# First chunk in two halves: the values' products of two row blocks moved ahead of the queries

## The chip, the cores and the metric

One core of a Trainium2 chip runs the kernel. The metric is the device time of one execution in microseconds; the program uses no other core. Engines: TensorE (PE, matmuls and transposes; PEld its weight loads), VectorE (DVE), ScalarE (ACT), GpSimd (POOL) and SyncE (SP, which here only issues DMAs).

## What is computed

```python
def _A_ref(x, wqkv, wo):                      # full attention, S=2048, D=512, 32 heads of 16
    qkv = (x @ wqkv) ...                      # q, k, v
    p = softmax(einsum(q, k) * Dh ** -0.5)
    return einsum(p, v) ... @ wo

def _B_ref(x, w1, b1, w2, b2):                # token mixer, F=1792
    h = layernorm(x)
    u = gelu(einsum("bsd,sf->bdf", h, w1) + b1)
    return transpose(einsum("bdf,fs->bds", u, w2) + b2)

xn = layernorm(x)
out = x + _A_ref(xn, A_wqkv, A_wo) * silu(_B_ref(xn, B_w1, B_b1, B_w2, B_b2))
```

All tensors are float32.

## The kernel before

The whole kernel has one order, written out by hand: each engine, and each DMA queue, takes its instructions in the order in which the program issues them. Every product is made of three: operands are split into an upper part (`wh`, or index 0 of a tile), rounded to the reduced float32 format, and a lower part (`wl`, index 1), the rest, and upper by upper, upper by lower and lower by upper are added in PSUM. ACT makes upper parts by a cast, DVE (from PSUM) or GpSimd (from SBUF) makes lower parts by a subtraction (`sub`, line 76).

The first stage works on the 2048 rows of x in four chunks of 512 rows, each of four row blocks of 128. For a chunk it does the following.

- `load_x` (line 162) loads four blocks; `first(c)` normalises them with `Norm` (lines 193 to 231): statistics of each block (`stats`), one reciprocal root for all four (`rsqrt`, of which one step is on ACT), then the four blocks scaled (`apply`, line 219).
- `turned(c, db)` (lines 261 to 269) transposes one column block of all four row blocks on PE into one PSUM bank, and ACT (line 267) and DVE make its two parts, tile `xt`. A chunk has four column blocks, so four such tiles.
- Eight groups of twelve matmuls (line 300) make the queries (four groups) and then the keys (four). A group takes the four upper weight slices with the upper rows, then the same with the lower rows, then the four lower weight slices with the upper rows. ACT and DVE split each result into `sg` (line 305), of which there are three buffers, and it is stored. Between the groups stand two at a time the pieces of `todo`: the normalisation of the next chunk, and the second normalisation of this chunk (`second`), whose results `hx` are split by ACT (line 243) and GpSimd into `hu`, for the mixer.
- The values of four row blocks (`v_product`, lines 83 to 85) follow, 48 matmuls, with the next chunk's transposes among them. Their results go by ACT (line 354) to `v48` tiles of two buffers, in which GpSimd has set the ones (line 353), and are stored to `v_d` (line 355).

In the first chunk the weights have to be brought in as well. Twelve slices (three parts: queries 0, keys 1, values 2; four slices `kd` each) are loaded in this order (line 182) into eleven buffers, so the tenth waits until the first has been used up. `w_upper` (line 187) casts a part's slices on ACT, `w_lower` (line 191) subtracts them on GpSimd. The loads of the two bias vectors are issued behind those of chunk 1's rows (lines 289, 290), and DVE has one small operation on the second vector (`b2h`, line 291) ahead of everything that it does in the loop for chunk 0.

PSUM has eight banks, handed out in turn by `bank()`. Behind the four chunks come the mixer's products and the attention, which fill the rest of the span.

Of the kernel before, what the change touches and what calls it, by code (L numbers as in the profile page):

```python
# [8 lines left out]
F32 = mybir.dt.float32  # L9
F32R = mybir.dt.float32r  # L10
AF = mybir.ActivationFunctionType
OP = mybir.AluOpType
# [9 lines left out]
def tile_attention_token_mixer(ctx, tc, x, wqkv, wo, w1, b1, w2, b2, out):  # L22
# [128 lines left out]
    with (  # L151
        tc.tile_pool(name="pw", bufs=1) as pw,
        tc.tile_pool(name="px", bufs=5) as px,
        tc.tile_pool(name="pt", bufs=6) as pt,
        tc.tile_pool(name="pst", bufs=3) as pst,
# [29 lines left out]
        def w_upper(part):  # L185
            for kd in range(ND):
                nc.scalar.copy(wh[part][:, kd, :], raw_w[part, kd])

        def w_lower(part):
            for kd in range(ND):  # L190
                sub(nc.gpsimd, wl[part][:, kd, :], raw_w[part, kd], wh[part][:, kd, :])

        class Norm:


            def __init__(self, src, dst, then=None):
                self.src, self.dst, self.then = src, dst, then
                self.st = pst.tile([P, 4, 6], F32, name="st")
                self.mv = pst.tile([P, 4, 2], F32, name="mv")
# [5 lines left out]
            def rsqrt(self):  # L205
                ve = pst.tile([P, 4], F32, name="ve")
                r = self.r = pst.tile([P, 4], F32, name="r")
                t = pst.tile([P, 4], F32, name="t")
                nc.vector.tensor_scalar(ve, self.mv[:, :, 1], 1e-5, None, op0=OP.add)
# [16 lines left out]
            def pieces(self):  # L226
                for b in range(4):
                    yield lambda b=b: self.stats(b)
                yield self.rsqrt
                for b in range(4):  # L230
                    yield lambda b=b: self.apply(b)

        def first(c):
# [4 lines left out]
            return Norm(lambda b: xr[4 * c + b], dst)  # L238

# [15 lines left out]

        for f in first(0).pieces():
            f()
        w_upper(0)
        xts_ = [[] for _ in range(NC)]

        def turned(c, db):

            ps = bank()
            for b in range(4):
                nc.tensor.transpose(ps[:, b * P : (b + 1) * P], xn[4 * c + b][:, db * P : (db + 1) * P], ident)
            t = pt.tile([P, 2, 512], F32R, name="xt")
            nc.scalar.copy(t[:, 0, :], ps)
            sub(nc.vector, t[:, 1, :], ps, t[:, 0, :])
            xts_[c].append(t)

        for c in range(NC):
            cs = slice(c * 512, (c + 1) * 512)
            for db in range(len(xts_[c]), ND):
# [12 lines left out]
            if c == 0:  # L286
                w_upper(2)
                w_lower(2)
                nc.sync.dma_start(b1t, b1.rearrange("(b p) -> p b", p=P))
# [46 lines left out]

            pv = [bank()[:, :D] for _ in range(4)]
            if c + 1 < NC:
                for kd in range(ND):
                    for b in range(4):  # L340
# [3 lines left out]
            for b, ps in enumerate(pv):  # L344
                if c + 1 == NC:
# [4 lines left out]
                else:  # L350
                    v48 = pt.tile([P, 2, 512], F32R, name="xt").bitcast(F32).rearrange("p a b -> p (a b)")
                    v48 = v48[:, : NP * 48].rearrange("p (a b c) -> p a b c", b=3, c=DH)
                nc.gpsimd.memset(v48[:, :, 1, :], 1.0)
                nc.scalar.copy(v48[:, :, 0:3:2, :], ps.rearrange("p (a b c) -> p a b c", b=2, c=DH))
                nc.sync.dma_start(v_d[4 * c + b], v48.rearrange("p a b c -> p (a b c)"))

# [732 lines left out]
```

## Time and profile before

| | before |
|---|---|
| median of 3 runs | 1708.67 us (1707.78 to 1708.83) |
| the profiled execution's own time | 1709.11 us |
| its span in the profile | 1707.3 us |
| PE, DVE, ACT, POOL busy | 98%, 83%, 70%, 33% of the span |
| PE clock granted, mean | 0.995 |
| first transpose on PE | 9.65 us |
| first product of queries, chunk 0 | 13.61 us |
| first product of values, chunk 0 | 36.97 us |
| first product of queries, chunk 1 | 48.92 us |

The span runs from the first to the last recorded instruction; the execution's own time has some 1.8 us around it. In the timeline a row gives start, duration, engine, line and operation, `out<-in`, and in brackets how long the engine was idle before it and what ended that. Starts of neighbouring matmuls tell more than their durations, which overlap.

### The profile page before, as it was taken

Reading aid. Unit: us, or ns where it says so; the run is one execution under the profiler, and the core shown is the slowest. Engines: PE = TensorE matmul, PEld = TensorE weight load, DVE = VectorE, ACT = ScalarE, POOL = GpSimd, SP = SyncE. Lnnn points to the kernel's source line nnn. Section 1 sums busy time; section 2 is a strip of 40 time slices with the busy share of each in tenths; the row PEclk is TensorE's granted clock in tenths of the full one; section 3 lists DMA queues with packets and bytes.
Section 4 is the critical chain, followed back from the end, with each engine's and each line's share of the span. In section 5 each row is a group of like instructions: output and inputs, shape, how many; then the busy total and the mean of one; then the engine's idle time right before and its main releaser. Section 6 shows DMA issues by size and latency. Waiting matters only on the chain.

```text
span 1707.3 us, 30652 instructions
## 1 busy us (share of the span) xinstructions
PE 1672.8 (98%) x11716; PEld 846.9 (50%) x11716; DVE 1409.7 (83%) x2378; ACT 1187.9 (70%) x2291; POOL 567.1 (33%) x673
## 2 busy tenths in 40 slices
PE   7999999999999999999999999999999999999987
PEld 6887644444444444444444444444444444444443
DVE  6565888888888888888888888888888888888834
ACT  3333277777777777777777777777777777787845
POOL 4223842233342334333422322222222222463401
PEclk9999999999999999999999999999999999999999
DMA  6467611415150514353332415141515132272435
GB/s 222 179 235 184 133 44 42 75 44 85 45 85 20 92 46 68 135 127 94 75 60 64 79 35 82 36 80 31 81 33 82 37 48 52 78 158 85 147 98 186
DMA packets 150879, 152.94 MB, mean 90 GB/s; under 512 B 51452, under 2 KB 109820, under 8 KB 147660
## 3 DMA queue, kind: packets, MB, share of 16 engines
q1 hardware_dynamic: 146188, 149.97, 36.8%
q0 software_dynamic: 4544, 1.01, 0.4%
q8 instruction: 92, 1.51, 0.4%
q14 instruction: 55, 0.45, 0.1%
HBM read 100.29 MB, written 49.53 MB: 88 GB/s over the span
## 4 chain that ended last, share of the span: by engine, by line
PE 92%; DVE 5%; ACT 1%; DMA 0%; issue 0%; POOL 0%; SPq 0%; DVEq 0%; POOLq 0%
PE av L773 28%; PE dn L911 26%; PE mx L387 13%; PE sc L757 12%; DVE mxp L391 4%; PE dn L886 3%; PE mx L300 2%; PE sc L300 2%; ACT prob L762 1%; PE av L886 1%; PE av L300 1%; PE dn L300 1%; PE mx L757 1%; PE mx L402 0%; PE sc L83 0%
## 5 line engine op out<-in xcount | busy, mean ns | idle before, releaser
L391 DVE TENSOR_REDUCE mxp<-mx 128x1 f32<-128x512 f32 x2008 | 1250.5, 683 | 183.9 <-PE mx L387 97.4
L762 ACT ACTIVATE prob<-sc 128x512 f32<-128x512 f32 x2008 | 1041.8, 604 | 331.1 <-PE sc L757 252.6
L387 PE MATMUL mx<-big 48*128 48x512 f32 x2008 | 826.8, 428 | 2.1
L757 PE MATMUL sc<-big 50*128 50x512 f32 x2008 | 771.8, 428 | 3.4 <-DMA big<-m 2.0
L911 PE MATMUL dn<-hu,wh 64*128 64x512 f32 x1570 | 573.8, 406 | 0.0
L773 PE MATMUL av<-prob,vp 128*32 128x512 f32 x4096 | 546.3, 605 | 0.0
L387 PEld LDWEIGHTS mx<-big 48*128 48x128 f32 x2008 | 364.2, 186 | 221.8 <-DVE mxp L391 206.6
L757 PEld LDWEIGHTS sc<-big 50*128 50x128 f32 x2008 | 355.1, 185 | 191.7 <-ACT prob L762 173.3
L911 PEld LDWEIGHTS dn<-hu,wh 64*128 64x128 f32 x1570 | 289.3, 185 | 171.5 <-issue 145.5
L911 PE MATMUL dn<-hu,wl 64*128 64x512 f32 x786 | 316.3, 402 | 0.0
L145 POOL CAST wh<-raw 128x512 fp32r<-128x512 f32 x108 | 62.8, 582 | 327.3 <-PE dn L911 309.6
L76 POOL TENSOR_TENSOR wl<-raw,wh 128x512 fp32r<-128x512 f32 x124 | 150.3, 1215 | 38.6 <-ACT wh L147 29.9
L773 PEld LDWEIGHTS av<-prob,vp 128*32 128x32 f32 x4096 | 81.0, 108 | 150.6 <-issue 138.6
L911 PEld LDWEIGHTS dn<-hu,wl 64*128 64x128 f32 x786 | 145.9, 186 | 8.3 <-issue 0.8
L406 POOL CAST m<-f 16x128 fp32r<-16x128 f32 x32 | 9.0, 280 | 266.1 <-DVE f L405 266.1
L464 POOL TENSOR_TENSOR sq<-u 128x512 f32<-128x512 f32 x14 | 14.6, 1040 | 170.9 <-ACT u L463 170.9
L80 POOL DMA_DIRECT2D big<-m x128 | 67.7, 535 | 0.0
L762 ACT ACTIVATE prob<-mx 128x512 f32<-128x512 f32 x40 | 25.1, 627 | 29.2 <-PE sc L757 22.0
L500 POOL TENSOR_SCALAR t<-t 128x512 f32<-128x512 f32 x16 | 23.8, 1488 | 62.4 <-ACT t L497 62.4
L911 PE MATMUL dn<-wh,hu 64*128 64x512 f32 x120 | 41.6, 399 | 0.0
L76 POOL TENSOR_TENSOR hu<-hx,hu 128x512 fp32r<-128x512 f32 x16 | 20.4, 1291 | 54.6 <-ACT hu L243 54.6
L300 PE MATMUL mx<-xt,big 128*128 128x512 f32 x144 | 35.4, 395 | 0.0
(202 smaller groups left out, 1094.2 us busy)
## 6 DMA issues: line engine op xcount, KB each, us to landing
raw<-in_B_w_dram SPq DMA_DIRECT2D x104, 256.0 KB
big<-k_d SPq DMA_DIRECT2D x96, 128.0 KB
big<-q_d SPq DMA_DIRECT2D x96, 128.0 KB
q_d<-sg SPq DMA_DIRECT2D x16, 512.0 KB
k_d<-sg SPq DMA_DIRECT2D x16, 512.0 KB
num_d<-ev SPq DMA_DIRECT2D x30, 256.0 KB
u_d<-uo SPq DMA_DIRECT2D x14, 512.0 KB
hu<-u_d SPq DMA_DIRECT2D x14, 512.0 KB
```

The costliest lines, as they stand in the source:

```text
L76: eng.tensor_tensor(out=o, in0=a, in1=b.bitcast(F32), op=OP.subtract)
L80: queue.dma_start(dst.bitcast(F32), src.bitcast(F32))
L145: nc.gpsimd.tensor_copy(whs[n][:, :m, :], raws[n][:, :m, :])
L300: nc.tensor.matmul(ps, w[part][:, kd, m], xt[kd][:, z, :], start=w is wh and z == 0 and kd == 0, stop=w is wl and kd == ND - 1,)
L387: nc.tensor.matmul(ps, q[o : o + 48, r * P : (r + 1) * P], k[o : o + 48, c * 512 : (c + 1) * 512], start=True, stop=True,)
L391: nc.vector.tensor_reduce(mxp[u // 16][:, a, r % 8, c : c + 1], ps, axis=AX.X, op=OP.max)
L500: nc.gpsimd.tensor_scalar(t, t, 1.0, None, op0=OP.add)
L757: nc.tensor.matmul(ps, ks[p][o : o + 50, kb * P : (kb + 1) * P], qs[p][o : o + 50, at : at + 512], start=True, stop=True,)
L762: nc.scalar.activation(e, ps, AF.Exp, scale=scale)
L773: nc.tensor.matmul(av[32 * j : 32 * j + 32, :], vps[p][:, kb, 16 * a : 16 * a + 32], prob.pop((t, a, c)), start=kb == 0, stop=kb == NB - 1,)
L886: nc.tensor.matmul(ps, w(slice(0, P)), m(slice(0, P)), start=first, stop=last)
L911: made.append(lambda r=r, start=first and a == lead, stop=last and a != lead: nc.tensor.matmul(ps, w(r), m(r), start=start, stop=stop,))
```

## The change

The values' weights are loaded first, and split first. The first chunk's four row blocks are normalised as two pairs, each with a root of its own. Its blocks are turned one block at a time (all four column blocks of a row block into one bank) rather than one column block at a time, and cast in halves of 256 elements. Between the turns stand the values' products of the first two row blocks, 24 matmuls; then come the queries' weights, and the loop goes on as before, with values of only two blocks left at its end for chunk 0. The `xt` tiles become pairs, three buffers in place of six. The results of the two early blocks are copied and stored ahead of the bias vectors' loads.

```diff
-        tc.tile_pool(name="pt", bufs=6) as pt,
+        tc.tile_pool(name="pt", bufs=3) as pt,
...
-        for part in range(3):
+        for n, part in enumerate((2, 0, 1)):
             for kd in range(ND):
-                nm = ("raw", "wh", "wl")[(part * ND + kd) % 3]
+                nm = ("raw", "wh", "wl")[(n * ND + kd) % 3]
...
             def rsqrt(self):
-                ve = pst.tile([P, 4], F32, name="ve")
+                at = slice(self.some[0], self.some[-1] + 1)
+                ve = pst.tile([P, 4], F32, name="ve")[:, at]
...
-        for f in first(0).pieces():
-            f()
-        w_upper(0)
...
+            if db % 2 == 0:
+                t2 = pt.tile([P, 2, 2, 512], F32R, name="xt")
+                xts_[c] += [t2[:, 0], t2[:, 1]]
...
+        def block_turn(b):
+            ps = bank()
+            for db in range(ND):
+                nc.tensor.transpose(ps[:, db * P : (db + 1) * P], xn[b][:, db * P : (db + 1) * P], ident)
+            return ps
+        def block_upper(b, ps):
+            for h in range(2):
+                nc.scalar.copy(pair[h][:, :, 0, b * P : (b + 1) * P], ps[:, 256 * h : 256 * h + 256].rearrange("p (d q) -> p d q", d=2))
+        def block_lower(b, ps):
+            for h in range(2):
+                o = pair[h][:, :, :, b * P : (b + 1) * P]
+                sub(nc.vector, o[:, :, 1, :], ps[:, 256 * h : 256 * h + 256].rearrange("p (d q) -> p d q", d=2), o[:, :, 0, :])
+        def v_out(n, ps, v48, ones_in=False):
+            if not ones_in:
+                nc.gpsimd.memset(v48[:, :, 1, :], 1.0)
+            nc.scalar.copy(v48[:, :, 0:3:2, :], ps.rearrange("p (a b c) -> p a b c", b=2, c=DH))
+            nc.sync.dma_start(v_d[n], v48.rearrange("p a b c -> p (a b c)"))
...
+        halves_ = [first(0, range(2)), first(0, range(2, 4))]
+        pieces_ = [list(h.pieces()) for h in halves_]
+        for f in pieces_[0]:
+            f()
+        pair = [pt.tile([P, 2, 2, 512], F32R, name="xt") for _ in range(2)]
...
+        ps0 = block_turn(0)
+        w_upper(2, [0])
+        block_upper(0, ps0)
+        w_upper(2, [1])
+        pieces_[1][0]()
+        block_lower(0, ps0)
+        nc.gpsimd.tensor_copy(pst.tile([P, 1], F32, name="hold"), xn[1][:, :1])
+        w_lower(2, [0, 1])
+        ps1 = block_turn(1)
+        w_upper(2, [2])
+        block_upper(1, ps1)
+        w_upper(2, [3])
+        w_lower(2, [2, 3])
+        pieces_[1][1]()
+        block_lower(1, ps1)
+        for f in pieces_[1][2:]:
+            f()
+        pv = [bank()[:, :D] for _ in range(2)]
+        def v_part(b, z, w, first, last):
+            for kd in range(ND):
+                nc.tensor.matmul(
+                    pv[b], xts_[0][kd][:, z, b * P : (b + 1) * P], w[2][:, kd, :],
+                    start=first and kd == 0, stop=last and kd == ND - 1,
+                )
+        v_part(0, 0, wh, True, False)
+        v_part(0, 1, wh, False, False)
+        v_part(1, 0, wh, True, False)
+        ps2 = block_turn(2)
+        block_upper(2, ps2)
+        v_part(1, 1, wh, False, False)
+        ps3 = block_turn(3)
+        block_upper(3, ps3)
+        block_lower(2, ps2)
+        block_lower(3, ps3)
+        w_upper(0)
+        v_part(0, 0, wl, False, True)
+        v_part(1, 0, wl, False, True)
+        w_lower(0)
         for c in range(NC):
...
-            if c == 0:
-                nc.gpsimd.tensor_copy(pst.tile([P, 1], F32, name="hold"), xn[3][:, :1])
-                w_upper(1)
-                w_lower(0)
-                w_lower(1)
             xt = xts_[c]
...
             if c == 0:
-                w_upper(2)
-                w_lower(2)
+                w_upper(1)
+                w_lower(1)
+                for b in range(2):
+                    v_out(b, pv[b], v48s[b], True)
                 nc.sync.dma_start(b1t, b1.rearrange("(b p) -> p b", p=P))
                 nc.sync.dma_start(b2t, b2.rearrange("(b p) -> p b", p=P))
                 nc.vector.tensor_scalar(b2h, b2t, 0.5, None, op0=OP.mult)
...
-            pv = [bank()[:, :D] for _ in range(4)]
+            rest_ = range(2 if c == 0 else 0, 4)
+            pv = {b: bank()[:, :D] for b in rest_}
...
-                    for b in range(4):
+                    for b in rest_:
                         v_product(b, kd)
```

More of the change, by code (lines that the diff above doesn't have):

```diff
@@ L183, in tile_attention_token_mixer, with w_upper, w_lower, __init__ @@
                 raw_w[part, kd] = raw
-        def w_upper(part):
-            for kd in range(ND):
+        def w_upper(part, kds=range(ND)):
+            for kd in kds:
                 nc.scalar.copy(wh[part][:, kd, :], raw_w[part, kd])
-        def w_lower(part):
-            for kd in range(ND):
+        def w_lower(part, kds=range(ND)):
+            for kd in kds:
                 sub(nc.gpsimd, wl[part][:, kd, :], raw_w[part, kd], wh[part][:, kd, :])
         class Norm:
-            def __init__(self, src, dst, then=None):
-                self.src, self.dst, self.then = src, dst, then
+            def __init__(self, src, dst, then=None, some=range(4)):
+                self.src, self.dst, self.then, self.some = src, dst, then, some
                 self.st = pst.tile([P, 4, 6], F32, name="st")
@@ L226, in pieces, with first @@
             def pieces(self):
-                for b in range(4):
+                for b in self.some:
                     yield lambda b=b: self.stats(b)
                 yield self.rsqrt
-                for b in range(4):
+                for b in self.some:
                     yield lambda b=b: self.apply(b)
-        def first(c):
+        def first(c, some=range(4)):
             def dst(b):
@@ L236, in dst @@
                 return xn[4 * c + b]
-            return Norm(lambda b: xr[4 * c + b], dst)
+            return Norm(lambda b: xr[4 * c + b], dst, some=some)
         def second(c):
@@ new lines, in v_out @@
+        def v_out(n, ps, v48, ones_in=False):
[3 more added lines that the diff above has]
+            nc.sync.dma_start(v_d[n], v48.rearrange("p a b c -> p (a b c)"))
+        v48s = [pst.tile([P, NP, 3, DH], F32, name="v48", bufs=2) for _ in range(2)]
+        for v48 in v48s:
+            nc.gpsimd.memset(v48[:, :, 1, :], 1.0)
+        halves_ = [first(0, range(2)), first(0, range(2, 4))]
@@ new lines, in tile_attention_token_mixer @@
+        pieces_ = [list(h.pieces()) for h in halves_]
+        for f in pieces_[0]:
+            f()
+        pair = [pt.tile([P, 2, 2, 512], F32R, name="xt") for _ in range(2)]
+        xts_[0] = [pair[db // 2][:, db % 2] for db in range(ND)]
+        done_db[0] = ND
+        ps0 = block_turn(0)
[5 more added lines that the diff above has]
+        nc.gpsimd.tensor_copy(pst.tile([P, 1], F32, name="hold"), xn[1][:, :1])
@@ L271, in tile_attention_token_mixer @@
+        v_part(0, 0, wh, True, False)
[12 more added lines that the diff above has]
+        w_lower(0)
         for c in range(NC):
             cs = slice(c * 512, (c + 1) * 512)
-            for db in range(len(xts_[c]), ND):
+            for db in range(done_db[c], ND):
@@ L343, in tile_attention_token_mixer @@
                         turned(c + 1, kd + 1)
-            for b, ps in enumerate(pv):
+            for b in rest_:
                 if c + 1 == NC:
```

21 lines of the change are left out of this document (11 added, 10 removed).

## The prediction

> **What bounds the kernel now.** I read the page first (engine shares, the chain that ended last), then the timeline of the first 60 us, where all of the change lies, then the table by stretches.
>
> ```profile
> span 1707.3 us, 30652 instructions
> ...
> PE 1672.8 (98%) x11716; PEld 846.9 (50%) x11716; DVE 1409.7 (83%) x2378; ACT 1187.9 (70%) x2291; POOL 567.1 (33%) x673
> ...
> PE 92%; DVE 5%; ACT 1%; DMA 0%; issue 0%; POOL 0%; SPq 0%; DVEq 0%; POOLq 0%
> ```
>
> TensorE (PE) is busy for 98% of the span and makes up 92% of the chain that ended last. A shift of the point from which PE is busy without a break, or a gap put into it, therefore reaches the end of the kernel nearly one for one; work on other engines counts only where PE has to wait for it. Next the timeline of the start; its columns are start, duration, engine, line and operation.
>
> ```profile
> 4.97 0.18 DVE L203 BATCH_NORM_AGGREGATE mv<-st 128x2 f32<-128x6 f32 x1
> ...
> 7.29 0.18 DVE L203 BATCH_NORM_AGGREGATE mv<-st 128x2 f32<-128x6 f32 x1
> ...
> 8.96 1.92 DVE L219 TENSOR_SCALAR xn<-xr,mv,r 128x512 f32<-128x512 f32 x4
> ...
> 9.65 1.75 PE L265 MATMUL mx<-ident,xn 128*128 128x128 f32 x4 [9.65 <-DVE xn L219]
> ...
> 11.20 1.06 PE L265 MATMUL sc<-ident,xn 128*128 128x128 f32 x4
> ...
> 12.29 0.58 ACT L267 CAST xt<-sc 128x512 fp32r<-128x512 f32 x1 [0.27 <-PE sc L265]
> ...
> 13.61 3.68 PE L300 MATMUL mx<-xt,big 128*128 128x512 f32 x12
> ...
> 15.00 0.62 ACT L187 CAST big<-wl 128x512 fp32r<-128x512 f32 x1
> 15.52 0.62 ACT L187 CAST big<-raw 128x512 fp32r<-128x512 f32 x1
> ...
> 16.03 1.30 POOL L76 TENSOR_TENSOR big<-wh,big 128x512 fp32r<-128x512 f32 x1
> ...
> 17.13 2.88 PE L300 MATMUL dn<-xt,big 128*128 128x512 f32 x12
> 17.29 1.30 POOL L76 TENSOR_TENSOR big<-wl,big 128x512 fp32r<-128x512 f32 x1
> ...
> 19.85 2.88 PE L300 MATMUL av<-xt,big 128*128 128x512 f32 x12
> ```
>
> DVE computes statistics of four row blocks, the last ending with the aggregate at 7.29; the short chain for the reciprocal root follows and the four blocks are normalised from 8.96. PE's first transpose is at 9.65, the first product of queries at 13.61, the second group of twelve at 17.13, the third at 19.85. So a group costs 19.85 - 17.13 = 2.72 us, 0.227 us a matmul, while the first took 17.13 - 13.61 = 3.52 (part of it at a slow clock).
>
> From 9.65 PE has no gap up to chunk 1's first product, at 48.92:
>
> ```profile
> 36.18 0.60 PE L265 MATMUL mx<-ident,xn 128*128 128x128 f32 x4
> ...
> 36.62 0.60 PE L265 MATMUL dn<-ident,xn 128*128 128x128 f32 x4
> ...
> 36.97 0.48 PE L83 MATMUL av<-wvh,xt 128*128 128x512 f32 x1
> ...
> 45.09 0.59 ACT L267 CAST xt<-dn 128x512 fp32r<-128x512 f32 x1
> ...
> 45.56 0.60 ACT L267 CAST xt<-mx 128x512 fp32r<-128x512 f32 x1
> ...
> 46.38 0.59 ACT L267 CAST xt<-sc 128x512 fp32r<-128x512 f32 x1 [0.21 <-PE sc L265]
> ...
> 47.72 4.37 SPq L355 DMA_DIRECT2D v_d<-v  x4
> ...
> 48.92 2.88 PE L300 MATMUL mx<-xt,big 128*128 128x512 f32 x12
> 50.16 0.59 ACT L354 COPY v<-mx 128x512 f32<-128x512 f32 x1 [1.82 <-DMA v_d<-v]
> ...
> 51.13 0.58 ACT L354 COPY v<-sc 128x512 f32<-128x512 f32 x1 [0.38 <-DMA v_d<-v]
> ```
>
> The values' products of chunk 0 start at 36.97 and chunk 1's queries at 48.92. Between them lie 48 matmuls (10.9 us) and two transposed groups (1.1 us). This stretch is also where the late work of chunk 0 on DVE and ACT is hidden: the casts of chunk 1's turned rows run at 45.09, 45.56, 46.38 (the last one ready at 46.97), and PE needs the fourth of them at 48.92 + 3 x 0.227 = 49.60. The slack is 2.6 us, no more. Four transposes take 36.62 - 36.18 = 0.44 us here.
>
> **Part 1: the early start.** The first half needs two blocks only. Its last aggregate is the one at 4.97 in place of 7.29; with the same 8.96 - 7.29 = 1.67 to the first normalised block this gives 6.64, and with 9.65 - 8.96 = 0.69 PE starts at 7.33. That is 2.32 us won, if PE then runs on.
>
> It does not. Block 0's four transposes take 1.06 to the end (11.20 row) and the cast follows 0.03 later (12.29), at 8.42. ACT now has, in this order: two half casts of block 0, weight slice 1, slice 2, two half casts of block 1, slice 3. Weight casts stand 15.52 - 15.00 = 0.52 apart, whole PSUM casts 45.56 - 45.09 = 0.47. A half cast (256 elements) has no row; it lies between half of that, 0.24, and all of it, and I take 0.30, near the lower end, because the elements are halved. So slice 3 is ready at 8.42 + 4 x 0.30 + 3 x 0.52 = 11.2. The first three products slip in before; nine of the first twelve are left. At 0.227 us they end at 13.2, at the slow clock (0.453, twice that) at 15.3; I take 14.0, since the trace's own first group shows the slow clock going after some 5 us of PE work. The weights' slices load first now, so they are there no later than the queries' were. The second half is not what PE waits for: its root stands on DVE behind block 1's lower part, which follows block 1's casts, so it begins near 11.2, and PE can turn block 2 from 11.2 + 1.67 + 0.69 = 13.6. Then block 2 turned 0.44, four products 0.9, block 3 turned 0.44, eight products with the lower weights 1.8: PE is ready for the queries at 17.6.
>
> Here a wait takes the place of the old one. The cast of the queries' weights now stands on ACT behind block 3's casts (15.9 to 16.5), so its first slice is ready at 17.1; GpSimd makes the lower parts one after the other, 17.29 - 16.03 = 1.26 apart, so the fourth is there at 17.1 + 5.0 = 22.1, and the second group starts at 22.5. Before it started at 17.13: 5.4 later. Against that stand the 24 matmuls that are already done, 24 x 0.227 = 5.4. The PE side of the change is worth 0, between -0.8 and +1.3 by the two clocks.
>
> **Part 2: what is moved behind it on the queue of SP.** The stores of the first two blocks' values now stand ahead of the loads of b1 and b2, and DVE has the small operation on b2 (line 291) ahead of all its work for chunk 0.
>
> ```profile
> 15.61 0.42 SPq L289 DMA_DIRECT2D b1t<-in_B_b_dram  x1
> ...
> 16.08 3.57 SPq L290 DMA_DIRECT2D b2t<-in_B_b_dram  x1
> ...
> 22.31 1.30 DVE L291 TENSOR_SCALAR b2h<-b2t 128x16 f32<-128x16 f32 x1 [7.00 <-DMA b2t<-in_B_b_dram]
> ```
>
> DVE waited 7.00 us for b2 already, to 22.31, and only then began the subtractions of the finished groups. In the table by stretches (per engine busy us, then clock, DMA share and GB/s) b2's tiny elements show as a busy DMA share at almost no GB/s:
>
> ```profile
> 18.00:19.00 1.00, 1.00 (x6) 0.81 (x6) 0.00 (x0) 1.00 (x3) 1.00 (x2) 1.00 1.02 377
> ...
> 19.50:20.00 0.50, 0.50 (x4) 0.42 (x3) 0.00 (x0) 0.00 (x0) 0.50 (x2) 1.00 1.21 117
> ...
> 20.50:21.00 0.50, 0.50 (x4) 0.39 (x3) 0.00 (x0) 0.14 (x1) 0.50 (x1) 1.00 0.86 6
> ...
> 22.00:22.50 0.50, 0.50 (x4) 0.42 (x3) 0.19 (x1) 0.00 (x0) 0.50 (x2) 1.00 0.00 0
> ```
>
> At 18 to 19 the DMA still moves 377 GB/s of x and weights, at 19.5 to 20 a third of that, at 20.5 to 21 it is 0.86 busy at 6 GB/s, and at 22 it is idle. So b1 and b2 are moved behind the bulk ahead of them, from a little after 19 on, in about 2.9 us.
>
> After the change: ACT's eight weight casts for queries and keys last from 16.5 to 20.7, the two copies of values to about 21.7. SP issues the first store at 21.3 and the second at 21.75, b1 at 22.2, b2 from 22.65. A store issued at 47.72 had landed by 50.16 (2.44 us, the buffer's next user), and the next by 51.13, 1.0 later; so the stores are through at 21.3 + 2.44 + 1.0 = 24.7, and b2 lands at 24.7 + 2.9 + 0.3 = 27.9. DVE's backlog starts 27.9 - 22.31 = 5.6 us late. Bounds: 4.3, an estimate with ACT and the loads each some 0.65 quicker; 6.6 if b2 takes as long from b1's issue as before, 22.31 - 15.61 = 6.7, which gives 28.9; and 1.3 more at the slow clock.
>
> Who waits for that? Behind the operation on b2 are queued eight subtractions for queries and keys, all of the normalisation of chunk 1 and the second normalisation of chunk 0, then the lower parts of chunk 1's turned rows. That queue has no room:
>
> ```profile
> 30.00:36.00 6.00, 6.00 (x28) 4.95 (x28) 5.90 (x14) 1.77 (x3) 0.00 (x0) 1.00 0.73 273
> ```
>
> 5.90 of 6.00 us busy. It depends on ACT, GpSimd and its own stores, not on PE, which is ahead of it. So it moves as a block: the last cast of turned rows, ready at 46.97 before, is ready at 46.97 - 0.35 + 5.6 = 52.2 (0.35 is the wait on PE in the row of 46.38, and the tighter spacing, which fall away). PE meanwhile comes to chunk 1 at 48.9 as before: 22.5, seven groups, two turned groups, 24 matmuls instead of 48. It needs the fourth cast for its fourth product, 3 x 0.227 = 0.68 into the group: the group in effect starts at 52.2 - 0.68 = 51.5. PE loses 51.5 - 48.9 = 2.6 us. The later banks, weights and buffers are free before that (eight banks for eight groups; the keys' lower weights are ready near 22.1 + 4 x 1.26 = 27.1 and needed near 30.7). From here the order is as before and DVE has room again, so nothing is given back and nothing more lost.
>
> **Part 3: the clock behind the gap.** The gap is from about 49 to 50.8, with only one product in half a microsecond until 52.2. The kernel has one gap like it:
>
> ```profile
> 205.10 0.39 PE L911 MATMUL dn<-hu,wl 64*128 64x512 f32 x1
> 207.49 0.47 PE L757 MATMUL sc<-big 50*128 50x512 f32 x1 [1.99 <-DMA big<-m]
> ...
> 209.63 0.77 PE L911 MATMUL dn<-hu,wh 64*128 64x512 f32 x1
> ...
> 212.76 0.55 PE L757 MATMUL sc<-big 50*128 50x512 f32 x1
> ...
> 213.62 0.40 PE L387 MATMUL mx<-big 48*128 48x512 f32 x1
> ```
>
> PE had nothing from 205.49 to 207.49 (the wait of 1.99). Matmuls ran at 0.39 before; from 209.63 to the end of the row of 212.76 they take 0.55 to 0.77, then 0.40 again. These are 3.5 us at, by those durations, about half the rate: 1.7 us lost, after only 2.0 us of idling. The new gap is as long and followed by a thin stretch; I take the 1.7, and keep 0 as the other end. The Trainium skill, page "TensorE: Matmul & The Clock Gate", section "Part 1: The HAM clock gate", says that the clock falls after at least one idle window of about 3.4 us. By that rule this gap would cost nothing beyond itself, and the sum would stay at +2.6; the rows above speak against it.
>
> Sum: 0 + 2.6 + 1.7 = +4.3. Against the profiled execution's own 1709.11 (span 1707.3 and 1.8 around it) that is 1713.4; the median of the runs lies 0.44 lower, so 1713.0.
>
> **The rivals.** *No slow clock behind the gap*: +2.6, 1711.3. For it: activity is thinned, not absent, after 50.8, and if PE's waits at 20 to 22 slow the clock there, that loss is swallowed by the later gap. Against it: the rows at 207.49.
> *DVE is not late enough* (the other side): if b2 lands by 22.31 + 2.6 + 0.35 = 25.3, the slack covers it, PE has no gap at 49, and the PE side alone is left: 0, 1708.7, not slower. It decides on how fast small elements follow the stores; for it speaks that less bulk is ahead of them (two stores in place of four loads of x and three weight slices), against it that b2's issue begins only at 22.65 and the elements alone need 2.9.
> *The early start is kept*: if also the queries' lower weights came in time, or PE's cold stretch fell into the waits, up to 2.3 are won: 1706.4. Against it: GpSimd's four times 1.26 after ACT's late cast.
> *A cold start*: thin work from 7.33 to 11.2 keeps the clock slow to 15.3; ACT's chain, b2 and DVE all move 1.3: +5.6, 1714.3.
>
> **How the numbers follow.** The forecast 0.48, no slow clock 0.25, not late enough 0.12, early start kept 0.07, cold start 0.08. What a measurement of this kernel can tell from no change is about 0.2%, 3.4 us. The forecast, +3.0 to +5.3 by the bounds of b2, lies mostly above that (0.40 of 0.48), no slow clock mostly below (0.08 above); with the cold start, slower is 0.56. Of the early start and of errors that I don't see 0.05 go to faster; 0.39 remain. The range goes from 1708.0, which takes in most of "not late enough", to 1715.6, the late bounds of b2 with the slow clock; the forecast's own range is 1711.7 to 1714.0.
>
> **What would show it.** In the profile after: PE's first transpose near 7.3; the first query group stretched to about 22.5 by waits for GpSimd's lower weights; DVE idle for about 10 us before line 291's operation, which starts near 28; a PE gap of 2 to 3 us near 49, released by ACT's casts of turned rows, and slow matmuls within 4 us behind it. It is wrong if b2 is there before 25, if PE has no gap near 49, or if the first query group ends before 20.

## The result, and the profile after

The changed kernel takes 1711.29 us (median of 17 runs, 1708.79 to 1713.6) where the kernel before takes 1707.73 (17 runs, 1706.15 to 1709.79): 1.0021 times as long, 95% interval 1.0013 to 1.0028. That is 3.6 us more, where 4.3 were forecast (on a median of 1708.67 from three runs; on 1707.73 the same 4.3 gives 1712.0). The profiled execution's own time is 1711.11. From the page after, its span, its engines and the chain that ended last:

```profile
span 1709.3 us, 30670 instructions
...
PE 1675.8 (98%) x11716; PEld 847.2 (50%) x11716; DVE 1412.4 (83%) x2388; ACT 1187.6 (69%) x2296; POOL 567.0 (33%) x673
...
PE 91%; DVE 5%; ACT 1%; issue 1%; POOL 1%; DMA 1%; SPq 0%; DVEq 0%; POOLq 0%
```

TensorE is still busy for 98% and still most of the chain, so the end still moves with whatever PE loses at the start. The timeline of the start, after the change (start, duration, engine, line and operation; in brackets the idle time before and its releaser):

```profile
5.03 0.18 DVE L203 BATCH_NORM_AGGREGATE mv<-st 128x2 f32<-128x6 f32 x1
...
7.37 1.09 PE L279 MATMUL mx<-ident,xn 128*128 128x128 f32 x4 [7.37 <-DVE xn L221]
...
11.03 0.65 ACT L187 CAST wvh<-raw 128x512 fp32r<-128x512 f32 x1
...
11.59 1.27 POOL L76 TENSOR_TENSOR wvl<-wl,wvh 128x512 fp32r<-128x512 f32 x1
...
11.73 2.50 PE L330 MATMUL mx<-wvh,xt 128*128 128x512 f32 x5 [0.27 <-ACT wvh L187]
...
11.86 1.02 DVE L211 TENSOR_SCALAR ve<-mv 128x2 f32<-128x2 f32 x1
12.81 1.27 POOL L76 TENSOR_TENSOR wvl<-raw,wvh 128x512 fp32r<-128x512 f32 x1
...
13.15 0.17 DVE L213 RECIPROCAL r<-t 128x2 f32<-128x2 f32 x1 [0.27 <-ACT t L212]
13.35 0.75 DVE L214 TENSOR_TENSOR t<-r 128x2 f32<-128x2 f32 x1
...
15.73 0.79 PE L279 MATMUL mx<-ident,xn 128*128 128x128 f32 x4
...
22.92 1.28 POOL L76 TENSOR_TENSOR big<-wh,big 128x512 fp32r<-128x512 f32 x1
...
24.25 0.51 PE L375 MATMUL av<-xt,big 128*128 128x512 f32 x1 [0.72 <-POOL big L76]
...
24.59 2.91 PE L375 MATMUL sc<-xt,big 128*128 128x512 f32 x12
...
29.15 0.17 DVE L366 TENSOR_SCALAR b2h<-b2t 128x16 f32<-128x16 f32 x1 [9.78 <-DMA b2t<-in_B_b_dram]
```

The first aggregate ends the first half at 5.03 and PE turns at 7.37, 2.28 us earlier than before. Then the gain runs out. Five products start from 11.73 and the next row stands at 14.03, so each takes 0.46 where 0.227 is the full pace. The two short steps of the second root, at 11.86 and 13.35, take 1.02 and 0.75 where such a step takes 0.16, and each ends as GpSimd's subtraction beside it ends (12.86 and 14.08); the reciprocal between them, at 13.15, takes only 0.17 beside the second of these subtractions. Block 2 is turned only at 15.73, without a wait of PE, as the slow products last until then. The fourth lower slice of the queries' weights ends at 24.20, PE, which has waited 0.72 for it, goes on at 24.25, and the second group starts at 24.59, 7.46 later than before (17.13). The operation on b2 comes at 29.15, after a wait of 9.78 on its DMA. Then the timeline around the end of chunk 0:

```profile
43.66 0.60 PE L264 MATMUL av<-ident,xn 128*128 128x128 f32 x4
...
44.63 0.69 DVE L76 TENSOR_TENSOR sg<-dn,sg 128x512 fp32r<-128x512 f32 x1
...
45.24 0.99 DVE L221 TENSOR_SCALAR hx<-xn,mv,r 128x512 f32<-128x512 f32 x2
...
47.83 1.96 DVE L221 TENSOR_SCALAR hx<-xn,mv,r 128x512 f32<-128x512 f32 x2 [1.60 <-POOL hu L76]
...
49.36 1.14 ACT L245 CAST hu<-hx 128x512 fp32r<-128x512 f32 x2 [2.41 <-DVE hx L221]
...
51.05 3.95 PE L375 MATMUL mx<-xt,big 128*128 128x512 f32 x12
...
51.84 0.61 ACT L269 CAST xt<-sc 128x512 fp32r<-128x512 f32 x1
...
53.57 0.99 PEld L375 LDWEIGHTS mx<-xt,big 128*128 128x128 f32 x5 [0.30 <-DVE xt L76]
...
54.83 2.88 PE L375 MATMUL dn<-xt,big 128*128 128x512 f32 x12
```

After the last key group PE starts to turn chunk 1 at 43.66. Four blocks of chunk 0's second normalisation (`hx`, line 221) are still to be done by DVE behind that group's subtraction (44.63), with a wait of 1.60 on GpSimd between the two pairs, and ACT's casts of them (49.36) stand ahead of its casts of chunk 1's turned rows. The fourth of these is ready at 51.84 + 0.61 = 52.45. PE comes to chunk 1 near 51.0, and its first group takes 54.83 - 51.05 = 3.78 instead of 2.72, with PE's weight loads waiting 0.30 at a time. There is no gap of 2.6 us and no slow clock (the granted clock is 1.00 in every microsecond from 46 to 59).

I call the start of chunk 0's second query group m1 and that of chunk 1's second query group m2. Between them every kernel does the same work on PE but for the 24 matmuls that the change moves ahead. m1 went from 17.13 to 24.59 (+7.46, of which 24 x 0.227 = 5.45 is work done earlier: +2.01 lost), m2 from 51.64 to 54.83 (+3.19: the 2.01, and 1.18 of stretch). The ends of the two profiled executions lie 2.0 apart (spans 1709.3 and 1707.3), the medians 3.6; the runs of one kernel scatter by up to 4.8, so what the rest of the kernel adds to m2's 3.19 can't be told from scatter.

### The profile page after: what moved, and what is told of

Its sections match the earlier page's. It is cut to its first block, busy times and chain, and to the rows that moved or that the text cites. A ratio compares the mean times of both kernels' runs of the same rounds, so it can differ in the third digit from the quotient of the medians.

```text
span 1709.3 us, 30670 instructions
## 1 busy us (share of the span) xinstructions
PE 1675.8 (98%) x11716; PEld 847.2 (50%) x11716; DVE 1412.4 (83%) x2388; ACT 1187.6 (69%) x2296; POOL 567.0 (33%) x673
## 4 chain that ended last, share of the span: by engine, by line
PE 91%; DVE 5%; ACT 1%; issue 1%; POOL 1%; DMA 1%; SPq 0%; DVEq 0%; POOLq 0%
PE av L849 28%; PE dn L987 26%; PE mx L463 13%; PE sc L833 11%; DVE mxp L467 4%; PE dn L962 3%; PE mx L375 2%; PE sc L375 2%; ACT prob L838 1%; PE mx L833 1%; PE av L962 1%; PE dn L375 1%; PE av L375 1%; PE mx L478 0%; DMA wh<-in_A_wqkv_dram 0%
```

## The experiments

All numbers in one table: *b2* is the start of the operation on b2, *turn* the start of the transposes behind the last key group, *4th cast* when the fourth cast of chunk 1's turned rows is ready. The second last column is m2 against 51.64; the last is the time against the kernel before on the same chip, with its interval (where there is none, one execution was measured).

| kernel | m1 | b2 | turn | 4th cast | m2 | +/- | time ratio |
|---|---|---|---|---|---|---|---|
| before | 17.13 | 22.31 | 36.18 | 46.97 | 51.64 | | 1 |
| after | 24.59 | 29.15 | 43.66 | 52.45 | 54.83 | +3.19 | 1.0021 [1.0013, 1.0028] |
| e1_bias_early | 23.96 | 19.92 | 43.03 | 51.83 | 54.20 | +2.56 | 1.0014 [1.0005, 1.0023] |
| e2_qweights_early | 21.89 | 26.63 | 40.93 | 49.84 | 52.22 | +0.58 | 1.0002 [0.9994, 1.0011] |
| e3_both_early | 21.18 | 20.20 | 40.22 | 49.01 | 51.39 | -0.25 | 0.9999 [0.9991, 1.0008] |
| e4_before_bias_late | 17.03 | 30.20 | 37.30 | 53.42 | 55.81 | +4.17 | 1.0018 [1.0009, 1.0027] |
| e5_pieces_early | 23.47 | 28.06 | 42.53 | 52.52 | 55.13 | +3.49 | 1712.16 against 1708.44 |
| e6_bias_pieces_early | 23.53 | 19.91 | 42.59 | 49.29 | 52.63 | +0.99 | 1.0018 [1.0008, 1.0027] |
| e7_three_early | 21.65 | 20.57 | 40.69 | 47.36 | 50.71 | -0.93 | 0.9997 [0.9988, 1.0006] |
| e8_warm | 23.26 | 28.94 | 42.31 | 52.15 | 54.52 | +2.88 | 1711.06 against 1708.44 |
| e9_hold | 22.11 | 26.81 | 41.18 | 50.04 | 52.41 | +0.77 | 1711.02 against 1707.62 |
| e10_warm_hold | 21.68 | 27.44 | 40.73 | 50.67 | 54.40 | +2.76 | 1714.16 against 1707.62 |
| e11_three_early_warm | 20.77 | 19.69 | 39.81 | 46.48 | 49.83 | -1.81 | 0.9995 [0.9986, 1.0004] |
| e12_before_warm | 17.13 | 23.07 | 36.18 | 47.01 | 51.65 | +0.01 | 1.0003 [0.9995, 1.0012] |

**First round: the two waits.** The expected texts name three theories. A: the later of two limits decides, PE's late start (2.0) and DVE's queue behind b2 (3.2). B: only PE's start counts. C: only b2 counts, which is the prediction's account, where PE comes to chunk 1 as before. None of them has the lost cover, the 24 matmuls fewer behind the last key group.

*e1_bias_early*: the loads of b1 and b2 ahead of the two stores.

```diff
-                for b in range(2):
-                    v_out(b, pv[b], v48s[b], True)
                 nc.sync.dma_start(b1t, b1.rearrange("(b p) -> p b", p=P))
                 nc.sync.dma_start(b2t, b2.rearrange("(b p) -> p b", p=P))
+                for b in range(2):
+                    v_out(b, pv[b], v48s[b], True)
```

> The changed kernel with the two bias loads issued ahead of the stores of the two early blocks' values, nothing else. Milestone: start of chunk 1's second query group (51.64 before the change, 54.83 after). Theory A (the later of two limits decides: PE, which reaches chunk 1 2.0 us late, and DVE's queue behind b2, which holds chunk 1's first group 3.2 us late): DVE's operation on b2 starts near 20, DVE's limit is gone, PE's stays: milestone 53.7, +2.0 against before. Theory B (only PE's start counts, DVE's wait is hidden): no change from after, 54.8. Theory C (only b2 counts): milestone 51.6, as before.

From its timeline, and from its table of waits (us in total, times, longest) on DVE between 24 and 52:

```profile
19.92 1.20 DVE L366 TENSOR_SCALAR b2h<-b2t 128x16 f32<-128x16 f32 x1 [1.19 <-DMA b2t<-in_B_b_dram]
```

```profile
DVE sg L76 <- ACT sg L380: 6.9, 7, 3.7
```

```profile
51.22 0.61 ACT L269 CAST xt<-sc 128x512 fp32r<-128x512 f32 x1
...
54.20 2.88 PE L375 MATMUL dn<-xt,big 128*128 128x512 f32 x12
```

b2 is in 9 us earlier, and DVE now has slack: it waits 6.9 us for ACT's casts of the finished groups, which follow PE. Yet the fourth cast is ready at 51.83 and the first group, from 50.42 to 54.20, still takes 3.78. m2 gains 0.63, all of which is already in m1. None of the three forecasts came (53.7, 54.8 and 51.6). C falls, and so does A as it stood: the stretch is there without a late b2. B's "no change" holds but for m1.

*e2_qweights_early* and *e3_both_early*: the queries' weights cast ahead of block 2's casts, and the hold that keeps GpSimd from starting on them too early; e3 is e1 and e2 together.

```diff
         for f in pieces_[1][2:]:
             f()
+        w_upper(0)
...
-        w_upper(0)
...
+        nc.gpsimd.tensor_copy(pst.tile([P, 1], F32, name="hold"), xn[3][:, :1])
         w_lower(0)
```

> The changed kernel with the upper cast of the queries' weights moved ahead of the casts of blocks 2 and 3 on ACT (into its idle time at 13 to 16.5), and their lower parts on GpSimd held until block 3 is normalised; the bias loads stay behind the stores but move with ACT, about 2 us earlier. First query group of chunk 0 ends near 22.3 in place of 24.6. Theory A: PE's limit falls to -0.2 against before, DVE's to +1.2: milestone 52.8. Theory B: 51.4. Theory C, b2 alone counts, gives 52.8 as well; it is told from A by the other runs.

> Both edits, bias loads early and queries' weights early. Theory A: both limits are gone, milestone 51.4, time as before the change (-0.2 us, within noise). If the profile's remaining loss is from something else (the slower clock in the values' products, the turned blocks), the milestone stays above 52.5.

m1 comes to 21.89 and 21.18, m2 to 52.22 and 51.39: 2.6 and 3.4 us better than after, and no longer to be told from before (1.0002 and 0.9999). For e2 52.8 or 51.4 had been expected, and neither came. The place of that one cast, with its hold, is most of what the change loses. But in e3, with b2 at 20.20, the first group of chunk 1 is still stretched: m2 - m1 is 30.21 there, 30.24 in after and in e1. The number forecast for e3 (51.4) was right by another mechanism than theory A's: m1 gained more than expected, and the stretch stayed.

*e4_before_bias_late*: the kernel before, with nine idle stores to a spare tensor on SP's queue ahead of b1 and b2.

```diff
+                for i in range(9):
+                    nc.sync.dma_start(spare_d[i], xn[i % 4])
                 nc.sync.dma_start(b1t, b1.rearrange("(b p) -> p b", p=P))
```

> The kernel before with nine extra stores of 256 KB (normalised blocks to a scratch tensor) put ahead of the two bias loads, so that b2 lands near 29 as it does after the change; PE's start is untouched. Theory A: DVE's queue decides alone, milestone 54.3 to 55, +2.7 to +3.4 us against before, nearly the whole cost of the change. A sum of two costs (PE's 2.0 and DVE's 1.1): +1.1, 52.8. Theory B: 51.6, no change.

From its timeline:

```profile
37.30 0.33 PE L266 MATMUL mx<-ident,xn 128*128 128x128 f32 x1 [1.07 <-DVE xn L220]
...
38.35 0.78 PE L266 MATMUL mx<-ident,xn 128*128 128x128 f32 x2 [0.72 <-DVE xn L220]
...
39.86 0.33 PE L266 MATMUL mx<-ident,xn 128*128 128x128 f32 x1 [0.73 <-DVE xn L220]
...
40.38 0.47 PE L84 MATMUL av<-wvh,xt 128*128 128x512 f32 x1
...
52.73 3.24 PE L303 MATMUL mx<-xt,big 128*128 128x512 f32 x12 [0.21 <-DVE xt L77]
52.81 0.61 ACT L268 CAST xt<-sc 128x512 fp32r<-128x512 f32 x1
...
55.81 2.90 PE L303 MATMUL dn<-xt,big 128*128 128x512 f32 x12
```

Nothing else is changed, b2's operation begins at 30.20, and m2 goes from 51.64 to 55.81 (A had 54.3 to 55). So lateness of b2 alone does cost, and theory B falls too. But most of the 4.17 is lost at another wait than the prediction's: DVE normalises chunk 1's rows so late that PE waits for them three times, 2.52 us in all, and the values' products start at 40.38 instead of 36.97, 3.41 later. Only the other 0.76 is lost at the casts. In after PE is some 7 us later at that point and has no such wait. The fourth cast is ready 23.2 behind b2. Two limits on it stand side by side, then: it is ready at the later of

- b2's operation + 23.2 (from e4): DVE works its queue down, waiting only for ACT and GpSimd;
- the turn behind the last key group + 8.8 (51.83 - 43.03 in e1, 49.01 - 40.22 in e3): the four blocks of second normalisation go through DVE, ACT and GpSimd in turn, ahead of ACT's casts.

In after they give 29.15 + 23.2 = 52.35 and 43.66 + 8.8 = 52.46, measured 52.45. In a later run where they don't, the later one decides: e8's b2 gives 52.14 and its turn 51.1, measured 52.15 (and e10, below). The 23.2 goes with an operation on b2 of 0.17; e12's takes 0.90, and 23.07 + 0.73 + 23.2 = 47.00, measured 47.01. In after they coincide, which is why taking away the one gains nothing.

**Second round: the two limits.** The theory's test is a pair. `per`, the pieces of normalisation run behind each group, is ceil(18 / 10) = 2, so four blocks' pieces stand behind the last group's subtraction; with 3 all 18 are done after the sixth group.

*e5_pieces_early* moves the pieces alone, *e6_bias_pieces_early* is e1 and e5, *e7_three_early* is e1, e2 and e5:

```diff
-            per = -(-len(todo) // (len(order) + 2))
+            per = 3 if c == 0 else -(-len(todo) // (len(order) + 2))
```

> The changed kernel, with three pieces of normalisation in place of two behind each query and key group of chunk 0, so that the second normalisation is over before the last groups; b2 stays late. New theory D: chunk 1's first group is stretched (3.9 in place of 2.7 us) because the work that follows the last key group on DVE, GpSimd and ACT (8.6 us from the turn behind that group to the fourth cast, the same in all four changed kernels so far) is covered by only 7.1 us of values' products; b2's lateness gives a second limit that happens to be as late (b2 at 29.15 plus 23.2 us, as with the late bias loads in the kernel before, is 52.4; measured 52.45). By D the total work on DVE behind b2 is unchanged here, so this edit alone gains nothing: milestone (chunk 1's second group) 54.3 to 54.9. If b2 is no limit at all: 53.7.

> As e5, and the bias loads ahead of the stores. By D both limits are now gone: chunk 1's first group takes 2.7 to 2.9 us again, its start to the start of the next, and the milestone is 29.2 us after the second query group of chunk 0 starts (30.2 in the changed kernel). If the stretch has another cause, the group stays at 3.7 or more.

> Bias loads early, queries' weights early and pieces early together. By D: milestone 50.2 to 50.5, 1.1 to 1.4 us less than before the change (51.64); time 0.06 to 0.08% below before, hardly told from it. If the stretch stays: 51.4.

The first two groups of chunk 1 on PE, in e5:

```profile
51.10 4.19 PE L375 MATMUL mx<-xt,big 128*128 128x512 f32 x12 [1.14 <-ACT xt L269]
55.13 2.90 PE L375 MATMUL dn<-xt,big 128*128 128x512 f32 x12
```

and in e6:

```profile
49.89 2.90 PE L375 MATMUL mx<-xt,big 128*128 128x512 f32 x12
52.63 2.88 PE L375 MATMUL dn<-xt,big 128*128 128x512 f32 x12
```

With the pieces alone PE even has a wait of 1.14 for the casts, and m2 - m1 is 31.66; m2 is later than expected (54.3 to 54.9). b2's limit does not carry over to that order: 28.06 + 23.2 = 51.26, measured 52.52, as DVE now waits twice 1.17 for ACT's casts of finished groups, which stand behind its casts of `hx`. With both moved, the first group takes 52.63 - 49.89 = 2.74, nothing is stretched, and m2 - m1 is 29.10 (29.06 in e7), as in before without the 24 matmuls: 34.51 - 5.45 = 29.06. Moving one limit gains 0 (e1: 30.24 as in after; e5: worse), moving both 1.14. That is the stretch, shown.

e6's m2 is 2.2 us better than after's, but its time is not: 1.0018. Part of it is lost further on, where PE waits for rows that GpSimd's DMA writes. First in after, then in e6, from the timeline of PE:

```profile
210.48 0.60 PE L833 MATMUL sc<-big 50*128 50x512 f32 x1 [1.78 <-DMA big<-m]
```

```profile
209.41 0.76 PE L833 MATMUL sc<-big 50*128 50x512 f32 x1 [2.88 <-DMA big<-m]
```

At this one place PE idles 1.78 in after and 2.88 in e6 (1.99 in before, in the prediction's row), and the granted clock falls to 0.50: in the traces' clock records for 3.4 us in before, after, e2, e3, e5, e7 and e8, for 6.8 us in the other seven. To see what it does I compared the start of DVE's 60th and 100th row-maximum reductions, which are the same work in every kernel, with those of before: +3.23 and +3.02 in after, +1.02 and +2.76 in e6, -0.20 and -0.82 in e3, -1.78 and -0.72 in e11, +0.02 and +1.70 in e12, +2.92 and +5.06 in e10. So this place adds up to 2.1 us or takes up to 0.6 whatever was won at the start, and the executions with 6.8 us all lose 0.7 or more at it; what decides it from run to run was not tried.

**Third round: the start-up.** m1 is 23.5 to 24.6 in the kernels with the change's start-up (after, e1, e5, e6). Theory: two things hold it, the slow pace of the first products and the normalisation of the second half, blocked by GpSimd. Rival: only one of them.

*e8_warm*: 30 transposes of the identity ahead, into a bank that is overwritten later, so that PE is not cold.

```diff
+        warm = ps_av.tile([P, 512], F32, name="av")
+        for _ in range(30):
+            nc.tensor.transpose(warm[:, :P], ident, ident)
         nc.scalar.preload_act_table(AF.Sqrt)
```

> The changed kernel with 30 transposes of the identity into an unused bank as PE's first work, from about 1.3 us, so that the clock is up when the real work starts. If the slow clock in the values' first products alone makes PE late, the second query group of chunk 0 starts 1.7 to 2.0 us earlier, at 22.7 in place of 24.6. If the second pair's normalisation (block 2 ready at 15.3, its small DVE steps of 1.02 and 0.75 us each ending with a GpSimd subtraction) is as late as the products, it starts at most 0.6 earlier, 24.0.

```profile
7.33 0.66 PE L282 MATMUL mx<-ident,xn 128*128 128x128 f32 x4 [0.17 <-DVE xn L224]
...
11.04 1.04 DVE L214 TENSOR_SCALAR ve<-mv 128x2 f32<-128x2 f32 x1
...
12.17 1.09 PE L333 MATMUL sc<-wvh,xt 128*128 128x512 f32 x4
...
14.55 0.66 PE L282 MATMUL mx<-ident,xn 128*128 128x128 f32 x4 [1.29 <-DVE xn L224]
```

Block 0 is turned in 0.66 instead of 1.09 and four products from 12.17 take 1.09, full pace. PE then waits 1.29 for block 2, until 14.55, since the root's first step still takes 1.04; m1 is 23.26, little better, and between the two numbers expected. A warm PE alone is hidden behind the normalisation.

*e9_hold*: GpSimd's last two lower slices of the values' weights wait until the second half is normalised.

```diff
-        w_lower(2, [2, 3])
         pieces_[1][1]()
         block_lower(1, ps1)
         for f in pieces_[1][2:]:
             f()
+        nc.gpsimd.tensor_copy(pst.tile([P, 1], F32, name="hold"), xn[3][:, :1])
+        w_lower(2, [2, 3])
```

> The changed kernel with GpSimd's lower parts of the values' slices 2 and 3 held until block 3 is normalised, so that nothing runs on GpSimd during the second pair's root. If GpSimd blocks DVE's small steps there, the steps of 1.02 and 0.75 us fall to 0.17 each and block 2 is ready 1.4 us earlier after block 1's lower part. The start of the second query group of chunk 0 hardly moves (23.0 to 24.0; 23.5 to 24.6 in the kernels without this edit), because PE is still busy with products at the slow clock.

```profile
11.36 0.16 DVE L211 TENSOR_SCALAR ve<-mv 128x2 f32<-128x2 f32 x1
...
11.99 0.16 DVE L214 TENSOR_TENSOR t<-r 128x2 f32<-128x2 f32 x1
...
13.41 0.63 PE L279 MATMUL mx<-ident,xn 128*128 128x128 f32 x4
```

The same two steps take 0.16 each and block 2 is turned at 13.41, 2.32 earlier than in after. Part of that is the pace of the products: in e5, where they ran as fast as here, block 2 was turned at 14.77, so holding GpSimd back is worth 1.4 (1.6 from e8 to e10, 14.55 to 12.98). I had expected the slow products to hide that (23.0 to 24.0), but m1 is 22.11: in this execution the same five products ran at full pace (1.43 for the five, 2.50 in after). The pace differs between executions that start alike, 2.50 in e2 and 1.42 in e3. The first clock record in the trace, a step to full speed, stands at 16.1 in after, 15.6 in e2, 10.5 in e3 and 10.4 in e9. So single values of m1 carry up to 1 us of chance: after, e1, e5 and e6, which open alike, have 24.59, 23.96, 23.47 and 23.53.

*e10_warm_hold* is e8 and e9.

> Both the 30 transposes ahead and GpSimd held. If the slow clock and GpSimd's blocking are two limits of which the later decides, the gain appears only now: block 2 is turned near 13.2 and the second query group of chunk 0 starts at 21.3 to 22.0, 1.3 to 2.0 us before that of the kernel with the transposes alone (23.26). If they add up instead, the kernel with one of them would have shown half of it.

m1 is 21.68 as expected, 2.91 less than in after. But m2 gains nothing, 54.40, as b2 is still late (27.44). From its timeline:

```profile
49.26 5.34 PE L379 MATMUL mx<-xt,big 128*128 128x512 f32 x12 [1.06 <-ACT xt L272]
...
51.04 0.68 DVE L76 TENSOR_TENSOR xt<-sc,xt 128x512 fp32r<-128x512 f32 x1
...
54.40 1.83 PE L379 MATMUL dn<-xt,big 128*128 128x512 f32 x7
```

and from its table by stretches (PE, PEld, DVE, ACT and POOL busy us, then granted clock, DMA share and GB/s):

```profile
51.00:52.00 1.00, 1.00 (x4) 0.76 (x4) 0.72 (x2) 0.64 (x2) 0.29 (x2) 0.57 0.00 0
...
53.00:54.00 1.00, 1.00 (x4) 0.71 (x4) 0.00 (x0) 0.00 (x0) 0.00 (x0) 0.50 1.06 354
```

Here the conditions are those that the prediction reckoned with: PE early, DVE's queue behind b2. b2's limit gives 27.44 + 23.2 = 50.64 (measured 50.67); PE has a gap of 1.06 and a thin stretch, and then the granted clock falls to 0.50, from 51.15 to 54.56 in the clock records. The group takes 54.40 - 49.26 = 5.14. DVE's last lower part is through at 51.04 + 0.68 = 51.72, and the next group starts 2.68 behind that; at full clock this took 54.83 - 53.51 = 1.32 in after and 54.52 - 53.21 = 1.31 in e8. So 1.4 us are lost to the clock.

But such a gap does not always bring the slow clock. e8 has one of nearly the same length, with the same thin stretch behind it:

```profile
50.75 3.94 PE L378 MATMUL mx<-xt,big 128*128 128x512 f32 x12 [0.97 <-ACT xt L272]
```

e5 has a longer one (1.14, its row above). In both the granted clock stays at 1.00 throughout, from 48 to 55. What sets e10 apart was not tried.

*e11_three_early_warm* is e7 with the 30 transposes, *e12_before_warm* the kernel before with 40.

> The three moves (bias loads, queries' weights, pieces early) and the 30 transposes ahead. Second query group of chunk 0 at 20.6 to 21.0 (21.65 without the transposes), the second group of chunk 1 at 49.7 to 50.1, 1.6 to 1.9 us less than before the change. The time of the whole follows within the 1 to 2 us by which PE's wait and slow clock near 205 us differ from kernel to kernel: 0 to -3 us.

> The kernel before the change with 40 transposes of the identity as PE's first work. Its first query group is then limited by GpSimd's lower weights (the fourth ready at 16.1) in place of the slow clock: the second query group starts at 16.4 to 16.6 in place of 17.13, the second group of chunk 1 at 50.9 to 51.1 (51.64), -0.6 us. If the clock mattered fully, 2 us.

e11 is the furthest that the change was brought: m1 20.77, m2 49.83, 1.81 us ahead of before. Its time, 1706.91 against 1707.62, can't be told from before's (0.9995, to 1.0004). e12 missed: m1 stayed at 17.13.

```profile
1.37 5.97 PE L178 MATMUL av<-ident 128*128 128x128 f32 x40 [1.37 <-POOL ident masks.py:199]
9.88 1.85 PE L268 MATMUL mx<-ident,xn 128*128 128x128 f32 x4 [2.54 <-DVE xn L222]
11.52 1.06 PE L268 MATMUL sc<-ident,xn 128*128 128x128 f32 x4
```

The 40 transposes were through at 7.34, since PE got fast during them; it then idled 2.54, the granted clock fell to 0.50 from 11.1 to 14.5, and the four transposes took 1.06 again, as cold as before (1.06 in the prediction's row). So e11 and e12 don't say what a warm start is worth to the kernel before.

## Why the prediction was right

The time was right, slower by about as much as forecast, and the road from the queries' weights and b2 to the end of chunk 0 was found. How near the sum came is in good part luck. Of its three terms only the middle one has the right kind, and none the right size: 0 + 2.6 + 1.7 stood for 2.0 + 1.2 + 0, and the errors of +2.0, -1.4 and -1.7 mostly cancel. The measured 1711.29 lies just below the forecast's own range (1711.7 to 1714.0). And one of the prediction's signs of being wrong came: PE has no gap near 49 in after, nor one longer than 0.35 later at chunk 1.

**The early start** held where its rows reached: the first aggregate (5.03), the first transpose (7.37, forecast 7.33), and that a wait for the queries' lower weights swallows the gain. The step that failed is "The PE side of the change is worth 0, between -0.8 and +1.3": it is +2.0 in after, and 1.4, 0.9 and 1.0 in e1, e5 and e6, which open alike. Slice 3 was ready at 11.68, not 11.2, the first twelve products were through at 15.7, not 14.0 (beyond the bound 15.3), and GpSimd's fourth slice came at 24.20, not 22.1. "The second half is not what PE waits for" (block 2 from 13.6) held in after only because the products were that slow: PE turned block 2 at 15.73 without a wait, but where the products ran at full pace it did wait for it (1.12 in e5, to 14.77, and 1.29 in e8). The second root runs beside GpSimd's subtractions, and two of its steps wait them out. e9 shows this, e8 that the pace alone isn't it, and e2, e3 and e7 what the late cast of the queries' weights costs (m1 of 21.2 to 21.9, against 23.5 to 24.6).

**b2** held: at 29.15 where 27.9 was forecast and 28.9 the bound, and DVE's backlog moved by 5.7 us, forecast 5.6 (the operation took 0.17 and not 1.30, which made up for part of its lateness). The fourth cast is ready at 52.45, forecast 52.2. e4 shows by itself that a late b2 moves DVE's queue and costs PE time, though there mostly at the transposes and only in part at the casts.

**The gap** was mis-sized: 2.6 forecast, 1.2 measured, and as a stretched group, not as a gap. The step that failed is "PE meanwhile comes to chunk 1 at 48.9 as before": it came near 51.0, as m1 was 2 us later than forecast. PE's lateness and DVE's overlap, so what the first term got too small the second got too large, and the sum of both, 2.6, stands against 3.2 measured. Not seen at all was the second limit: with 24 matmuls fewer, what PE covers behind the last key group is 24 x 0.227 + 4 x 0.44 = 7.2 us, not 12.7, and the tail of the second normalisation needs 8.8. "It depends on ACT, GpSimd and its own stores, not on PE" is true of before, but in e1 the same queue follows PE (6.9 us of waits for ACT).

**The slow clock** did not come: the granted clock is 1.00 throughout the thin stretch in after, where no wait is longer than 0.35 us. In e10, with a gap of 1.06 and what follows, it came and cost 1.4, forecast 1.7; in e5 and e8, with gaps of 1.14 and 0.97, it did not come. So the price is about right where the clock falls, but that a gap there makes it fall is not shown, and what decides it stays open. By the Trainium skill, page "TensorE: Matmul & The Clock Gate", section "Part 1: The HAM clock gate", the clock falls after at least one idle window of about 3.4 us; e5 and e8 agree, but e10 does not (1.06 idle), nor does the place near 207 (1.99 in before). The rival *no slow clock*, 1711.3, has the measured time, though not by its terms.

**The rivals.** *DVE is not late enough* fell: b2 was later than forecast. *The early start is kept* fell in after (m1 24.59), and e11 shows what it takes to keep part of it. *A cold start* was partly what happened: the slow pace went to 15.7 in after, and b2 came 1.3 later than forecast; in e3, e5 and e9 the step to full speed is on record at 10.4 to 10.9.

## What to carry to other kernels

Work moved ahead of a stage is not only earlier work: it is also cover taken away from whatever was hidden behind that stage, so count for each tail what still covers it. Where two waits end at the same time, undoing one shows nothing, and only the pair undone does; look for the second before calling the first harmless. And a load queued behind stores keeps everything behind its first use waiting, however small it is.

## What the runs showed of the hardware

Two-element steps of DVE (lines 211 and 214, 128x2 outputs) took 1.02 and 0.75 us beside a GpSimd subtraction and ended with it, 0.16 with GpSimd held back; the reciprocal between them (line 213) took 0.17 beside the same subtraction, so not every step is held. b2's operation took 1.30 in before and 0.17 in after. The Trainium skill, page "SBUF — State Buffer", section "Who interferes with whom", has the rule: one port pair is shared by DVE and GpSimd, who has it holds it for the whole instruction, and only DVE instructions that use that pair are blocked. The runs agree, and give it a price: block 2 turned 1.4 to 1.6 us later (e5 against e9, e8 against e10).

The granted clock fell to 0.50 after 1.06 us without a matmul and some 1.5 us of thin work in e10, but stayed at 1.00 with gaps of 1.14 and 0.97 at the same place in e5 and e8; so one such trace is no rule. Near 207 it fell in every trace, around waits of 1.5 to 3.3 us. And the first products of a cold PE started 0.46 or 0.25 us apart (after and e3), with 1.00 in the column of the granted clock both times: the trace has no clock record before the first step to full speed, at 16.1 and 10.5, so only the pace shows the slow start.
